# Order of the first loads and transposes, and the queue of the last store, in a gated linear-attention kernel

## The chip, the cores and the metric

The kernel runs on one core of a Trainium2 chip. The metric is the time of one execution in microseconds (us) as the device measures it.

## The reference, cut to what matters

```python
x = A_x                                             # (1, 2048, 1024) bf16
g = sigmoid((x * gate_w).sum(-1, keepdims=True))
a = linear_attention(x, A_wqkv, A_wo)               # 32 heads of 32; phi(q), phi(k), num / den, then @ wo
b = one_token_ffn(x, B_w_r, B_w_gate, B_w_up, B_w_down)   # FFN of the one token with the largest x @ w_r
return g * a + (1 - g) * b                          # (1, 2048, 1024) bf16
```

The start of the kernel computes K = x @ wk for the first two tiles of 128 tokens, for which x has to be transposed. The end writes the last 128 rows of the output.

## The kernel before

The transfers at the start, all from SyncE's queue. Tiles 0 and 1 of x come plain and are transposed on TensorE; later tiles are transposed by the transfer itself. A "K row" is 128 rows of the K weights (256 KB, as much as one x tile).

```python
load_x(0, 1)
load_k(0)
load_x(1, 1)
for c in range(1, KC):          # KC = 8
    load_k(c)
v_cut = D + 32 * (VH[0] + VH[1])
sp.dma_start(out=wkv[:, :, v_cut : 2 * D], in_=wqkv_v[:, :, D + v_cut : 3 * D])   # the V piece, 640 KB
...
```

TensorE's work on them, in program order. `warm` issues dummy matmuls that keep the array busy; `first_mm(t, c0, c1)` does two matmuls of 512 columns for each K row c of tile t.

```python
warm(N_WARM)                    # 6 dummies of 512 columns
...
unit_T(0)                       # 8 transposes of tile 0, copied out by VectorE and ScalarE
warm(3, 128)
first_mm(0, 0, 1)
wps = ps_ffn.tile([P, 16], BF, tag="f")
pe.transpose(wps[:], wrg_rows[:], ident[0:16, 0:16])     # router and gate rows
dve.tensor_copy(wkv[:, :, 2 * D : 2 * D + 2], wps[:].rearrange("p (w c) -> p c w", w=2))
unit_T(1)
for c in range(1, KC):
    first_mm(0, c, c + 1)
    if c < KC - 1:
        first_mm(1, c - 1, c)
...
for t in range(3):
    unit_V(t, 2, ps_t, "t")     # the first matmuls that need the V piece
```

The last row tile is computed and stored in three pieces of 512, 384 and 128 columns:

```python
for c0, cw in cols:
    ...                         # 8 matmuls
    dve.scalar_tensor_tensor(ot[:, c0 : c0 + cw], ps[:, 0:cw], gate[:, t : t + 1], xg[:, c0 : c0 + cw], ...)
    if t == NT - 1:
        nc.sync.dma_start(out=out2d[t * P : (t + 1) * P, c0 : c0 + cw], in_=ot[:, c0 : c0 + cw])
```

## Time and profile before

| | before |
|---|---|
| median of 6 runs (range) | 249.16 us (248.55 to 249.42) |
| span of the profiled run | 247.02 us |
| TensorE's share of the chain that ended last | 97% |
| first matmul of K row 1 / first V matmul | 6.54 / 13.01 us |
| end of VectorE's last instruction | 243.81 us |
| from there to the end of the span ("the tail") | 3.20 us |

TensorE has no gap worth the name from 1 us to 243 us. So a change can win only at what delays TensorE at the start, or in the tail. The prediction shows the lines.

### The profile page before, as it was taken

The page shows a single profiled execution, that of the slowest core. Times are in us where ns is not written, and L with a number is a line of the kernel's source. Part 1 is how long each engine was busy: PE and PEld are TensorE (multiplying, and loading weights), DVE is VectorE, ACT ScalarE, POOL GpSimd, SP SyncE. Part 2 cuts the span into 40 slices and gives each one's busy share as a digit, 9 for nine tenths or more (in the row PEclk, how much of TensorE's full clock was granted, in tenths as well). Part 3 has the DMA queues.
Part 4 walks back from the last instruction along what each step waited for, and adds up shares of the span by engine and source line. Part 5 has one row for each costly group of instructions (what it writes and reads, how often), then busy time and mean ns, then how long its engine had stood idle before and what let it go on. Part 6 is the DMA issues. An engine that isn't in the chain of part 4 may idle for free.

```text
span 247.0 us, 4867 instructions
## 1 busy us (share of the span) xinstructions
PE 240.8 (97%) x1898; PEld 123.6 (50%) x1923; DVE 172.7 (70%) x264; ACT 127.6 (52%) x215; POOL 52.5 (21%) x100
## 2 busy tenths in 40 slices
PE   8999999999999999999999999999999999999994
PEld 3466756654554554554554555544443444444442
DVE  0053124379984989845989999996789999954342
ACT  3195343355566376545555555668887633333300
POOL 6000000400000100000003300101666689950000
PEclk9999999999999999999999999999999999999999
DMA  6999995499969993599699690000004754464122
GB/s 207 343 239 195 267 392 151 108 326 337 281 194 292 341 290 88 149 312 384 224 345 340 230 280 3 3 4 21 0 3 127 204 182 148 155 190 166 48 82 86
DMA packets 46311, 47.78 MB, mean 193 GB/s; under 512 B 16776, under 2 KB 35472, under 8 KB 46224
## 3 DMA queue, kind: packets, MB, share of 16 engines
q1 hardware_dynamic: 45648, 46.28, 61.5%
q0 software_dynamic: 608, 1.19, 1.7%
q8 instruction: 15, 0.25, 0.5%
q14 instruction: 8, 0.07, 0.1%
q10 hardware_dynamic: 32, 0.00, 0.0%
HBM read 39.33 MB, written 8.39 MB: 193 GB/s over the span
## 4 chain that ended last, share of the span: by engine, by line
PE 97%; issue 1%; DVE 0%; DVEq 0%
PE ps L83 88%; PE first L83 3%; PE kvacc L83 2%; PE warm_ps L83 1%; PE red L83 1%; PE dps L83 1%; PE pst L83 1%; PE pm L83 1%; DVE ot L83 0%; PE yps L83 0%; PE pt L83 0%; DVEq L739 0%; PE hps L83 0%; PE rps L83 0%; PE wps L83 0%
## 5 line engine op out<-in xcount | busy, mean ns | idle before, releaser
L83 PE MATMUL ps<-wkv,xT 128*128 128x352 bf16 (+2 forms) x600 | 106.1, 334 | 0.4
L83 PEld LDWEIGHTS <-xT 128*128 128x128 bf16 x640 | 62.1, 98 | 49.1 <-issue 0.3
L83 ACT ACTIVATE u<-ps 128x512 f32<-128x512 f32 x60 | 35.9, 598 | 46.3 <-PE ps L83 45.7
L83 PE MATMUL ps<-xT,wq 128*128 128x512 bf16 x245 | 57.3, 379 | 0.6 <-issue 0.2
L83 PE MATMUL ps<-m_sb,pq_all 128*128 128x512 bf16 (+2 forms) x259 | 55.4, 373 | 0.3
L83 ACT ACTIVATE e<-u 128x512 f32<-128x512 f32 x64 | 40.3, 630 | 2.0
L83 PEld LDWEIGHTS <-pq_all 128*128 128x128 bf16 x264 | 25.4, 98 | 30.2 <-issue 0.7
L641 POOL TENSOR_TENSOR pq_all<-pq_all,rb 128x512 bf16<-128x512 bf16 x32 | 36.4, 1171 | 12.1 <-DVE rb L83 11.5
L83 PEld LDWEIGHTS <-wq 128*128 128x128 bf16 x256 | 24.5, 98 | 28.2 <-issue 1.0
L83 DVE SCALAR_TENSOR_TENSOR gacc<-wt,hcol,gacc 128x1024 f32<-128x1024 bf16 x27 | 34.5, 1278 | 0.4
L83 DVE SCALAR_TENSOR_TENSOR ot<-ps,gate,xg 128x512 bf16<-128x512 f32 (+2 forms) x33 | 23.9, 738 | 14.3 <-PE ps L83 13.1
L83 DVE SCALAR_TENSOR_TENSOR gacc<-wt,xs_f,gacc 128x2048 f32<-128x2048 bf16 x14 | 32.8, 2345 | 0.2
L83 ACT ACTIVATE xg<-xt,omg 128x1024 f32<-128x1024 bf16 x16 | 18.2, 1147 | 26.8 <-DVE ot L83 25.8
L83 DVE SCALAR_TENSOR_TENSOR pq_all<-ps,e 128x512 bf16<-128x512 f32 x32 | 21.9, 687 | 11.3 <-ACT e L83 11.3
L83 DVE SCALAR_TENSOR_TENSOR pk<-ps,e 128x512 bf16<-128x512 f32 x28 | 19.0, 686 | 11.8 <-ACT e L83 11.6
L83 DVE STREAM_SHUFFLE rb<-rdp 128x512 f32<-128x512 f32 x32 | 22.8, 753 | 0.0
L83 ACT CAST vt<-ps 128x352 bf16<-128x352 f32 x32 | 14.4, 453 | 11.4 <-PE ps L83 11.1
L214 POOL MEMSET vt<- 128x22 bf16 x16 | 3.7, 432 | 75.7 <-PE kvacc L83 75.2
L83 ACT CAST vc<-ps 128x320 bf16<-128x320 f32 x16 | 6.5, 428 | 7.3 <-PE ps L83 7.3
L83 DVE COPY rg<-ps 128x2 f32<-128x2 f32 x16 | 2.5, 159 | 10.2 <-ACT vc L83 10.1
L355 POOL DMA_DIRECT2D xs<-in_A_x_dram x1 | 0.7, 711 | 39.3 <-DVE sig L83 39.3
L83 DVE SCALAR_TENSOR_TENSOR pk<-first,e 128x512 bf16<-128x512 f32 x4 | 2.8, 692 | 7.9 <-ACT e L83 7.9
(100 smaller groups left out, 94.9 us busy)
## 6 DMA issues: line engine op xcount, KB each, us to landing
wt<-in_B_w_down_dram SPq DMA_DIRECT2D x14, 512.0 KB, 4.9
wt<-in_B_w_gate_dram SPq DMA_DIRECT2D x8, 512.0 KB, 7.6
wt<-in_B_w_up_dram SPq DMA_DIRECT2D x8, 512.0 KB, 8.3
xt<-xp SPq DMA_DIRECT2D x16, 256.0 KB, 2.7
out_dram<-ot SPq DMA_DIRECT2D x15, 256.0 KB, 2.0
wt<-in_B_w_gate_dram SPq DMA_DIRECT2D x8, 384.0 KB, 7.6
wt<-in_B_w_up_dram SPq DMA_DIRECT2D x8, 384.0 KB, 7.2
wkv<-in_A_wqkv_dram SPq DMA_DIRECT2D x8, 256.0 KB, 4.4
```

The lines of the kernel that those rows point to most:

```text
L83: inst = fn(*a, **k)
L214: nc.gpsimd.memset(vt_t[t][:, :, 32:33], 1.0)
L355: nc.gpsimd.dma_start(out=xs8[:], in_=x2d[bass.ds(idx_val, 1), :].rearrange("o (c p) -> (o c) p", p=P))
L641: nc.gpsimd.tensor_tensor(sl, sl, rb[:], op=ALU.mult)
```

## The change

Its intent: have both plain x tiles early, so that TensorE does all its transposes before the first K row is needed and never waits for tile 1; and let an idle engine issue the last store at once, where SyncE was still busy with the store before. The diff also moves the PSUM buffer (PSUM is TensorE's output memory) of the small transpose, `wps`, from the dummies' pool to that of the other transposes.

```diff
--- before.py
+++ after.py
@@ -134,9 +134,8 @@
         sp.dma_start(out=wkv[:, c, 0:D], in_=wqkv_v[:, c, D : 2 * D])
 
     load_x(0, 1)
-    load_k(0)
     load_x(1, 1)
-    for c in range(1, KC):
+    for c in range(KC):
         load_k(c)
     v_cut = D + 32 * (VH[0] + VH[1])
     sp.dma_start(out=wkv[:, :, v_cut : 2 * D], in_=wqkv_v[:, :, D + v_cut : 3 * D])
@@ -275,12 +274,13 @@
                 kv_mm(first[t][nb], t, nb, c, c + 1)
 
     unit_T(0)
-    warm(3, 128)
-    first_mm(0, 0, 1)
-    wps = ps_ffn.tile([P, 16], BF, tag="f")
+    wps = ps_t.tile([P, 16], BF, tag="t")
     pe.transpose(wps[:], wrg_rows[:], ident[0:16, 0:16])
     dve.tensor_copy(wkv[:, :, 2 * D : 2 * D + 2], wps[:].rearrange("p (w c) -> p c w", w=2))
+    warm(2, 128)
     unit_T(1)
+    warm(4, 128)
+    first_mm(0, 0, 1)
     for c in range(1, KC):
         first_mm(0, c, c + 1)
         if c < KC - 1:
@@ -703,7 +703,7 @@
             dve.scalar_tensor_tensor(ot[:, c0 : c0 + cw], ps[:, 0:cw], gate[:, t : t + 1],
                                            xg[:, c0 : c0 + cw], op0=ALU.mult, op1=ALU.add)
             if t == NT - 1:
-                nc.sync.dma_start(out=out2d[t * P : (t + 1) * P, c0 : c0 + cw], in_=ot[:, c0 : c0 + cw])
+                (nc.scalar if c0 + cw == D else nc.sync).dma_start(out=out2d[t * P : (t + 1) * P, c0 : c0 + cw], in_=ot[:, c0 : c0 + cw])
         if t < NT - 1:
             nc.sync.dma_start(out=out2d[t * P : (t + 1) * P, :], in_=ot[:])
         if t == 0:
```

## The prediction

> **What bounds the kernel now.** I read the page from the top: busy shares, then the chain that ended last, then the timeline of the first 14 us and of the last 5 us, because the diff touches only those two ends. The page says that TensorE is the bound nearly everywhere:
>
> ```profile
> span 247.0 us, 4867 instructions
> PE 240.8 (97%) x1898; PEld 123.6 (50%) x1923; DVE 172.7 (70%) x264; ACT 127.6 (52%) x215; POOL 52.5 (21%) x100
> ...
> PE 97%; issue 1%; DVE 0%; DVEq 0%
> ```
>
> The second line gives busy time and share per engine, the last one the chain of work that ended last by engine. TensorE has 97% of both, so what counts is what delays TensorE at the start, and what comes after its last matmul. The chain in order of time shows no gap over 0.1 us in the first 13 us:
>
> ```profile
> 1.02 2.72 PE warm_ps L83 x6
> 3.74 1.02 PE pst L83 x8
> 4.76 0.32 PE warm_ps L83 x3
> 5.08 0.85 PE first L83 x2
> 5.93 0.12 PE wps L83
> 6.05 0.59 PE pst L83 x8
> 6.64 4.59 PE first L83 x21
> ```
>
> Columns: start, us, what, count. The reader should divide. The two first matmuls of 512 columns take 0.85 us, 427 ns each (half clock). The 8 transposes of tile 0 take 1.02 us, 128 ns each with the last one's drain; those of tile 1 take 0.59 us, 74 ns each. So the array went over to full speed near 6.0 us; single starts of the second group, 80 ns and then 55 ns apart, say the same. From 6.54 us, when the matmul of K row 1 starts in the timeline, to 13.01 us, when the first V matmul starts, lie 30 matmuls (2 times 7 rows for tile 0, 2 times 8 for tile 1; one record is missing): 6.47 / 30 = 216 ns each, full speed with no stall. No later K row holds TensorE up.
>
> The arrivals come from the issue starts in the timeline plus the time to landing of each issue, taken in narrow windows of the tiles' view:
>
> ```profile
> 0.98 0.40 SPq L83 DMA_DIRECT2D xnat<-in_A_x_dram  x1
> 1.44 0.42 SPq L83 DMA_DIRECT2D wkv<-in_A_wqkv_dram  x1
> 1.90 0.45 SPq L83 DMA_DIRECT2D xnat<-in_A_x_dram  x1
> 2.39 3.75 SPq L83 DMA_DIRECT2D wkv<-in_A_wqkv_dram  x8
> ```
>
> x tile 0 lands 2.7 us after its issue, at 3.68 (TensorE starts on it at 3.72); K row 0 2.8 after, at 4.24; x tile 1 3.8 after, at 5.70; K row 1 4.1 after, at 6.49; row 2 4.3 after, at 7.16; row 7 5.7 after, at 10.9. Each is there before its use (tile 1 at 5.98, row 2 at about 7.4, row 7 at about 11.7), except row 1: it lands at 6.49 and its matmul starts at 6.54. It is the one transfer that TensorE just about waits for: the last transpose of tile 1 starts at 6.42 and would have let it start at about 6.48.
>
> The other end is the timeline after 242.3 us:
>
> ```profile
> 242.94 0.88 DVE L83 SCALAR_TENSOR_TENSOR ot<-ps,gate,xg 128x384 bf16<-128x384 f32 x2 [0.49 <-PE ps L83]
> ...
> 243.58 0.33 SPq L706 DMA_DIRECT2D out_dram<-ot  x1
> ...
> 244.01 0.38 SPq L706 DMA_DIRECT2D out_dram<-ot  x1
> ```
>
> The first line is two VectorE instructions, 242.94 to 243.56 and 243.56 to 243.82. The middle piece goes out at 243.58, 0.02 us after its data. The last piece goes out at 244.01, 0.19 us after its data, because SyncE is still at the middle one until 243.91 and needs some 0.1 us more. The DMA view gives 1.5 us from issue to landing for the last piece and 1.6 for the middle one: landings at 245.5 and 245.2. The span ends 1.5 us later, with nothing else of the kernel.
>
> **What the Trainium skill says.** "TensorE: Matmul & The Clock Gate", Part 1: the array starts at half clock and is let up to full after about 3.4 us of sustained work, in a free-running window, so the moment changes from run to run; it is a budget of time and not of matmuls. The trace agrees with the two speeds (427 and 216 ns for 512 columns); the change of speed comes 5.0 us after the first matmul, which fits a window that began some time after it. The same page gives N/2.4 + 2.5 ns for a matmul of N columns at full speed, 216 ns for 512, as measured here. "DMA: Bandwidth & Descriptors", Issuing engines are not separate DMA queues: issuing from another engine saves only the sequencer's issue time. That is the change at the end, and the trace shows that time as 0.33 to 0.38 us an issue. The same page, Anatomy of one DMA, puts most of the fixed 2 us of a transfer into confirming the last byte; the 1.5 us of this 32 KB piece fits, and another queue doesn't shorten it.
>
> **The change part by part.** Start, transfers: x tile 1 and K row 0 change places in one queue; both are 256 KB. So I give x tile 1 the old landing of row 0 (4.24) and row 0 the old one of tile 1 (5.70). Row 1 and all later ones keep theirs, as the bytes ahead of them are the same.
>
> Start, TensorE: moved are the small transpose of the router rows (it cost about 0.26 us, from the end of the matmuls before it at 5.72 to 5.98) and the 8 transposes of tile 1, now ahead of the first two K matmuls. Added are 6 dummy matmuls of 128 columns in place of 3: 3 x 128 = 384 columns more. Nothing useful is removed. The new path, at half clock 107 ns for 128 columns: tile 0's transposes 3.72 to 4.57; router transpose to 4.83; two dummies to 5.04; tile 1's transposes, 8 x 107, to 5.90 (their second PSUM buffer is freed by ScalarE's copy, which ends at 5.37, and is needed at about 5.47: no wait); then four dummies, one at half clock and three at full (56 ns), to about 6.17; then two K matmuls of row 0, 2 x 216 = 0.43, to 6.60. Row 0 is there at 5.70. Row 1's matmul starts at 6.60 instead of 6.54: 0.06 us later. From there the same 30 matmuls follow at 216 ns. The effect is bounded on both sides. As row 1 lands at 6.49 in both, nothing can start earlier than 6.53: the gain is at most 0.01 us. And the extra work is 384 columns, 0.16 us at full clock, which is what it costs if the clock goes up late (the work done before that moment is the same in both, and what is left over is done at full clock). So the start costs 0.06, between 0 and 0.16.
>
> Router copy: VectorE's copy of the router columns comes earlier, between the two tiles' copies; VectorE is idle there, so nothing.
>
> End: ScalarE has nothing left to do, and can start the last issue some 0.03 us after the data, at 243.85 instead of 244.01: 0.16 us saved. The landing is at 245.35 instead of 245.5, still after the middle piece at 245.2, so all of it shows. Another 0.15 is the most that could come beyond it, as the middle piece then ends last.
>
> Sum: +0.06 - 0.16 = -0.10 us, 0.04%: 249.1 becomes 249.0.
>
> **The rivals.** (1) The small transpose waits for its own data, as it now comes a microsecond earlier (4.57 instead of 5.86). For it: its weight load shows 0.84 us idle put down to "issue", and starts 0.14 us after the array was free, so something the profile doesn't name may have held it. Against it: the packets of that ScalarE queue are all moved by 3.1 us in the DMA view, and other transfers were done a few tenths after their last small packet. If it did wait until 5.8, TensorE would idle 1.2 us and might go over to full speed later: 250 to 251 us. I give this one in twelve. (2) x tile 1 lands later than 4.24, say at 5.3, since the queue serves several transfers at once. Then tile 1's transposes end at 6.1 and the start costs 0.2 us more. (3) The two queues share what makes descriptors, so the last piece gains nothing, or ScalarE's issue is slower (its first took 0.58 us, its second 0.28, against 0.40 for SyncE's first): the end then gives 0 and the total is 249.2. (4) Early data keeps TensorE busier in the runs in which the clock goes up early. There the kernel before waits for tile 1 until 5.70; but then both versions wait for row 1 at 6.49, so it gives nothing. (5) The order of instructions in the middle, which the program leaves partly free, comes out differently in the build. TensorE is 97% busy there, so that would cost or give tenths, but I can't see it from the profile.
>
> **Range and chances.** The three runs before lie between 249.04 and 249.42, so the moment of the clock and the chip alone make 0.2 either way, and my working spans -0.3 to +0.4. That gives 249.0, with 248.4 to 249.7 for 8 in 10. A 2% change is 5 us, more than all that happens outside TensorE's gapless stretch at both ends (the start before K row 1 is 6.5 us, the end after the last matmul some 3.5). Faster by over 2% 0.01, within 2% 0.98, slower 0.01.
>
> **What would show it.** In the profile after: x tile 1 landing near 4.3 and K row 0 near 5.7; row 1 still near 6.5; its first matmul between 6.5 and 6.7; the first V matmul 6.47 us after that; the last output issued from ScalarE's queue some 0.03 us after VectorE's last instruction, inside SyncE's issue of the middle piece; and the span from the end of VectorE's last instruction shorter by 0.16 from 3.2 us. I am wrong if row 1 itself lands earlier or later, if a gap appears before the small transpose or tile 1's transposes, if the clock goes up at another moment in a regular way, or if the middle of the kernel is ordered anew.

## The result, and the profile after

| | before | after |
|---|---|---|
| median of 6 runs (range) | 249.16 us (248.55 to 249.42) | 249.11 us (248.74 to 249.61) |
| span of the profiled run | 247.02 us | 247.48 us |
| first matmul of K row 1 | 6.54 us | 6.78 us |
| first V matmul | 13.01 us | 13.38 us |
| end of VectorE's last instruction | 243.81 us | 244.27 us |
| tail | 3.20 us | 3.21 us |

The ratio is 1.000, with a 95% interval of 0.9984 to 1.0017: the same.

The page of the changed kernel, busy times and the chain by engine:

```profile
span 247.5 us, 4896 instructions
PE 242.8 (98%) x1926; PEld 124.3 (50%) x1926; DVE 172.7 (70%) x264; ACT 127.6 (52%) x215; POOL 52.6 (21%) x100
...
PE 98%; DVE 0%; DVEq 0%; issue 0%
```

TensorE still bounds it. (Its 28 instructions more are mostly records that the trace before lacks: the program has 3 dummies more.) The chain in order of time, to be held against the seven lines in the prediction:

```profile
3.74 0.99 PE pst L83 x8
4.73 0.12 PE wps L83
4.85 0.33 PE warm_ps L83 x2
5.18 0.85 PE pst L83 x8
6.03 0.43 PE warm_ps L83 x4
6.46 6.96 PE first L83 x32
```

Both groups of transposes now take 0.85 us or more, so both run at half clock. The first K matmul follows all of them, at 6.25 us. The V matmuls then wait, which the kernel before did not show (timeline, weight loads; the bracket is the idle time ahead and what ended it):

```profile
13.38 0.66 PEld L83 LDWEIGHTS <-xT 128*128 128x128 bf16 x6 [0.45 <-DMA wkv<-in_A_wqkv_dram]
```

The end of the changed kernel (SPq and ACTq are the issuing sides of SyncE and ScalarE):

```profile
243.40 0.88 DVE L83 SCALAR_TENSOR_TENSOR ot<-ps,gate,xg 128x384 bf16<-128x384 f32 x2 [0.49 <-PE ps L83]
244.04 0.33 SPq L706 DMA_DIRECT2D out_dram<-ot  x1
244.31 0.39 ACTq L706 DMA_DIRECT2D out_dram<-ot  x1
```

The last issue starts 0.03 us after VectorE's end at 244.27 and inside SyncE's issue, as predicted. The span nevertheless ends 3.206 us after VectorE, against 3.205 before.

One profile of each kernel says little here: the two differ by 0.46 us, the medians by 0.05 the other way. So the experiments were read by the times of a few events in each trace. Each row below is one trace. "Full clock" is the moment at which the trace's record of the clock begins, which agrees with the change in the spacing of matmuls (in one trace 427, 260, then 216 ns apart about 10.07 us). The V column is the first V matmul. From there to VectorE's end lie 230.8 to 231.0 us in all 14 traces, so what the start loses or gains arrives at the end.

| kernel | K row 1 landed | its first matmul | full clock | V landed | V | VectorE's end | tail |
|---|---|---|---|---|---|---|---|
| before | 6.49 | 6.54 | 6.09 | 12.95 | 13.01 | 243.81 | 3.20 |
| before_again | 7.06 | 7.10 | 5.92 | 13.23 | 13.57 | 244.49 | 3.19 |
| end_only | 6.73 | 6.78 | 6.43 | 12.90 | 13.25 | 244.16 | 3.20 |
| after | 6.62 | 6.78 | 6.44 | 13.34 | 13.38 | 244.27 | 3.21 |
| after_again | 6.57 | 7.01 | 6.85 | 12.93 | 13.49 | 244.38 | 3.20 |
| after_third | 6.54 | 6.58 | 5.38 | 13.12 | 13.16 | 243.94 | 3.21 |
| start_only | 6.72 | 6.76 | 4.56 | 12.86 | 13.24 | 244.10 | 3.20 |
| no_dummies | 6.76 | 6.80 | 4.97 | 12.89 | 13.28 | 244.20 | 3.23 |
| more_dummies | 7.21 | 8.34 | 6.76 | 13.35 | 14.82 | 245.71 | 3.21 |
| order_only | 6.25 | 6.70 | 4.71 | 12.78 | 13.18 | 244.07 | 3.19 |
| swap_only | 6.60 | 7.86 | 10.07 | 13.15 | 15.43 | 246.44 | 3.20 |
| swap_filled | 7.45 | 7.88 | 5.44 | 13.42 | 14.39 | 245.26 | 3.20 |
| two_act | 7.21 | 7.25 | 6.70 | 13.24 | 13.72 | 244.57 | 2.96 |
| all_act | 6.93 | 6.98 | 4.03 | 13.33 | 13.45 | 244.34 | 2.85 |

### The profile page after: what moved, and what is told of

It is laid out like the page before. It is cut to its first block, busy times and chain, and to the rows that moved or that the text cites. A ratio compares the mean times of both kernels' runs of the same rounds, so it can differ in the third digit from the quotient of the medians.

```text
span 247.5 us, 4896 instructions
## 1 busy us (share of the span) xinstructions
PE 242.8 (98%) x1926; PEld 124.3 (50%) x1926; DVE 172.7 (70%) x264; ACT 127.6 (52%) x215; POOL 52.6 (21%) x100
## 4 chain that ended last, share of the span: by engine, by line
PE 98%; DVE 0%; DVEq 0%; issue 0%
PE ps L83 88%; PE first L83 3%; PE kvacc L83 2%; PE warm_ps L83 1%; PE red L83 1%; PE pst L83 1%; PE dps L83 1%; PE pm L83 1%; DVE ot L83 0%; PE yps L83 0%; PE pt L83 0%; DVEq L739 0%; PE hps L83 0%; PE rps L83 0%; PE wps L83 0%; PE xs_ps L83 0%
## 5 line engine op out<-in xcount | busy, mean ns | idle before, releaser
L83 PE MATMUL ps<-xT,wq 128*128 128x512 bf16 x256 | 58.3, 379 | 0.0
```

What stands on the lines that cost most here:

```text
L83: inst = fn(*a, **k)
```

## The experiments

The theory at this point: the start costs the dummies' columns and is otherwise ruled by chance (the moment of the clock), and in the tail something later than the landing swallows the gain. Rivals: the change itself moves the clock; the later K and V landings in its profile belong to it; the tail does gain and the single trace hides it. All outputs are right.

### Both kernels again: before_again, after_again

No edit. Five rounds each, together with the next two.

> The kernel before, unchanged, once more. Theory 'chance': the moment at which the array goes to full clock wanders by itself by some tenths of a us or more (6.1 in the first profile of this kernel, 6.4 in that of the changed one), and each us of it is worth 0.5 us of time; so this copy shows another moment than 6.1, and the end of VectorE's last instruction less half of that moment stays at 240.77 within 0.1. The tail after it stays 3.20. Rival 'the change moves the clock': this copy shows 6.1 again within 0.1. Ratio 1.000 within 0.002.

> The changed kernel, unchanged, once more. 'Chance': the clock goes up at another moment than 6.44; end of VectorE's last instruction less half of that moment is 241.05 as in the first profile if the 0.4 us later landings of K row 7 and the V piece (11.38 and 13.34 against 10.96 and 12.95) belong to the change, and about 240.93 (the 384 dummy columns alone, 0.16) if they were chance. 'The change moves the clock': 6.4 again. Ratio 1.000 within 0.002.

Measured: medians 248.99 and 249.17 us; ratios to the kernel before 0.9978 (0.9942 to 1.0013) and 0.9978 (0.9943 to 1.0013). The intervals are wide because two of the 11 runs of the kernel before took 251.02 and 250.91 us. The changed kernel went to full clock at 6.85 instead of 6.44 us. So the moment wanders with no change of the program; over all traces it lies between 4.0 and 6.9 where TensorE had no long gap before it. The later landings were chance, too: the V piece landed at 12.93 in this trace of the changed kernel and at 13.23 in that of the kernel before.

The reckoning "half of the clock's moment plus a constant" fell: the kernel before ends at 244.49 with a clock at 5.92, which gives 241.54 and not 240.77. (after_again gives 240.95, near the 240.93 expected of chance, but a reckoning that fails for one kernel supports nothing for the other.) The reason is in its timeline:

```profile
5.88 0.18 PE L83 MATMUL wps<-ident,wrg_rows 16*128 16x16 bf16 x1
6.24 0.62 PE L83 MATMUL pst<-ident,xnat 128*128 128x128 bf16 x8 [0.18 <-DMA xnat<-in_A_x_dram]
7.10 6.63 PE L83 MATMUL first<-wkv,xT 128*128 128x512 bf16 x29 [0.24 <-DMA wkv<-in_A_wqkv_dram]
```

The first bracket shows a wait for x tile 1, which landed at 6.20 instead of 5.68. That wait is what the change is meant to remove. The second bracket shows a further wait for K row 1, which makes the first one harmless: with tile 1 early, TensorE would have waited for K row 1 all the same.

### One part each: start_only, end_only

The changed kernel with the old end, and the kernel before with the new one:

```diff
# start_only, against after
-                (nc.scalar if c0 + cw == D else nc.sync).dma_start(out=out2d[...
+                nc.sync.dma_start(out=out2d[...
# end_only, against before: the opposite
```

> The start of the change with the old end. My sum of the start is a cost of 0.16 us for the dummy columns and up to 0.13 for a wait at the first V matmul: ratio 1.0006 to 1.0012, hardly to be told from 1. End of VectorE's last instruction less half of the clock's moment 240.93 to 241.05. The tail after it 3.20, the last issue 0.19 us after the data.

> The end of the change with the old start. My prediction: the last issue 0.03 us after its data and the tail 3.05 instead of 3.20, ratio 0.9994. Rival 'something later ends it': the last issue is 0.16 us earlier, but the tail is 3.20 again as in the changed kernel's first profile (3.206 against 3.205). End of VectorE's last instruction less half of the clock's moment 240.77, as before.

Measured: start_only 248.88 us, ratio 0.9976 (0.9942 to 1.0010); end_only 249.16 us, ratio 0.9993 (0.9958 to 1.0027). Neither is to be told from 1; the ratio of start_only lies below the 1.0006 to 1.0012 expected, inside the noise, and its VectorE end less half of the clock's moment is 241.83, outside the expected 240.93 to 241.05. The traces tell why. The chain of start_only, followed back from its end, leaves TensorE in the first microseconds and runs through one transfer:

```profile
1.90 0.45 SPq L83
2.35 0.04 issue
2.39 4.33 DMA wkv<-in_A_wqkv_dram
6.72 0.04 issue
6.76 4.05 PE first L83 x18
```

The third line is K row 1, issued at 2.39 and landed at 6.72. The array was at full clock by 4.56, TensorE was done with everything else, and the six dummies cost nothing. So the moment of the clock and the dummies count only where TensorE is later than that landing.

In end_only the last issue is 0.03 us after its data, and the tail is 3.196 us. The prediction for the end (3.05) is refuted, the rival (3.20) confirmed. The expectation for VectorE's end missed by 0.17 for the reason just told.

### What the dummies cost: more_dummies, no_dummies

```diff
# more_dummies, against after            # no_dummies, against after
     unit_T(1)                           -    warm(2, 128)
-    warm(4, 128)                             unit_T(1)
+    warm(28, 128)                       -    warm(4, 128)
     first_mm(0, 0, 1)                        first_mm(0, 0, 1)
```

> The changed kernel with 28 dummy matmuls of 128 columns after tile 1's transposes in place of 4: 24 x 128 = 3072 columns more. If a dummy costs its columns at full clock as I reckoned (24 x 56 ns = 1.33 us), the matmul of K row 1 starts 1.3 us later than the 6.8 to 7.0 of the changed kernel (at about 8.1 to 8.4), nothing waits for K rows or the V piece after that, and the whole is 1.1 to 1.3 us longer (ratio 1.005). If the start is bound by transfers and dummies are free, it starts by 7.1 and the ratio is 1.000.

> The changed kernel without its six short dummies. If 'the later of two' sets the start (K row 1's landing + 0.04 us, or TensorE's own work), the matmul of K row 1 now starts 0.04 us after that row lands, wherever that falls (6.5 to 7.1), so 0 to 0.3 us earlier than in the changed kernel: ratio 0.999 to 1.000, not to be told from 1. If the dummies are needed to bring the clock up, the array goes to full clock later than 7 us and the start is later than 7.1.

Measured: more_dummies 250.41 us, ratio 1.0051 (1.0031 to 1.0071), K row 1's matmul at 8.34; as expected. The 24 more dummies cost about their columns: the start moves by 1.33 to 1.56 us against after and after_again, 1.33 expected. no_dummies: K row 1 landed at 6.76 and its matmul started at 6.80, so the later of the two did set the start. Ratio 1.0027 (0.9990 to 1.0064), drawn up by one run of four at 250.77 us. Without the dummies TensorE idles:

```profile
4.87 0.68 PE L83 MATMUL pst<-ident,xnat 128*128 128x128 bf16 x8
6.15 7.29 PE L83 MATMUL first<-wkv,xT 128*128 128x512 bf16 x32 [0.60 <-DMA wkv<-in_A_wqkv_dram]
```

Here the array was already at full clock (4.97) and the 0.60 us did no harm. What such a gap does when it comes earlier is the next pair's subject.

### The two halves of the start: swap_only, order_only

```diff
# swap_only, against before: only the transfers
     load_x(0, 1)
-    load_k(0)
     load_x(1, 1)
-    for c in range(1, KC):
+    for c in range(KC):
# order_only, against after: old transfers and old end, new order and dummies on TensorE
```

> The kernel before with only the two transfers exchanged: x tile 1 ahead of K row 0, TensorE's order and dummies as before. Its first K matmuls come before tile 1's transposes and now wait for K row 0 until 5.4 to 6.0 instead of starting at 4.9; then 0.4 to 0.9 us of matmuls, 0.26 for the small transpose and 0.5 to 0.9 for tile 1: K row 1's matmul starts at 7.2 to 7.9, 0.4 to 1.1 us later than in the kernel before. Ratio 1.002 to 1.004. Rival 'exchange is free': by 7.1.

> The changed order of TensorE's work and its dummies with the old order of transfers and the old end. Tile 1's transposes are reached at 5.0 and wait for tile 1 until 5.4 to 6.2; then 0.5 to 0.9 us of transposes, 0.2 to 0.4 of dummies and 0.43 of matmuls: K row 1's matmul at 6.9 to 7.6, 0.1 to 0.6 us later than the changed kernel's 6.8 to 7.0. Ratio against before 1.001 to 1.002. So the two parts of the start are of use only together, and together give nothing over the kernel before.

Measured: swap_only 250.40 us, the four runs 251.18, 249.61, 251.25 and 248.53; ratio 1.0031 (0.9980 to 1.0083). K row 1's matmul came at 7.86, inside the expected range, yet VectorE ended at 246.44, 1.9 to 2.6 us later than in all traces but the two with many dummies. TensorE in that trace:

```profile
4.59 0.53 PE L83 MATMUL warm_ps<-const-bfloat16-1.0 128*128 128x128 bf16 x3
5.96 1.01 PE L83 MATMUL first<-wkv,xT 128*128 128x512 bf16 x2 [0.84 <-DMA wkv<-in_A_wqkv_dram]
6.91 0.19 PE L83 MATMUL wps<-ident,wrg_rows 16*128 16x16 bf16 x1
7.03 1.03 PE L83 MATMUL pst<-ident,xnat 128*128 128x128 bf16 x8
7.86 7.74 PE L83 MATMUL first<-wkv,xT 128*128 128x512 bf16 x30
```

The first K matmuls wait 0.84 us for K row 0. After it everything is at half clock (the transposes take 1.03 us), and stays so until 10.07. From 7.86 to the first V matmul at 15.43 lie 7.57 us, where other kernels need 6.47. That was not in my expectation. By the Trainium skill, "TensorE: Matmul & The Clock Gate", Part 1, the clock goes up after a busy window of some 3.4 us. My inference, which the page does not state, is that a gap inside a window puts the clock off by a whole one. 10.07 is 3.4 us past 6.66, a moment inside the 4.0 to 6.9 of the other traces, so it fits.

order_only: 249.26 us, ratio 1.0036 (0.9993 to 1.0080). It waits 0.42 us for tile 1, as expected, but its K row 1 matmul came at 6.70, below my 6.9: full clock was early (4.71). One of its four runs took 251.22 us.

### The gap filled, and the changed kernel once more: swap_filled, after_third

```diff
# swap_filled, against swap_only
-    warm(3, 128)
+    warm(12, 128)
```

> The kernel with only the two transfers exchanged, whose TensorE stood idle from 5.1 to 6.0 and went to full clock only at 10.1, now with 12 dummies of 128 columns in place of 3, which fill that idle time. Theory 'a gap loses a window': the array goes to full clock between 4.4 and 7.9 in each run, none is over 250.2 us, and the median is about 249.3 although it does more work than the exchange alone (median 250.4, two runs of four over 251). Rival 'the order itself is slow': median 250 or more, with some runs over 250.5 again.

> The changed kernel a third time, beside more runs of the kernel before. So far 2 of 36 runs with the old order of the start were over 250.5 us, and none of 18 with the new one and its dummies. If the new order guards against a lost window, none of these is over 250.2 and a few of the kernel before are; if the two were chance, both show some or none. Ratio 1.000 within 0.002; tail 3.20.

Measured: swap_filled 249.43 us (248.70 to 250.00), ratio 1.0014 (0.9997 to 1.0031). In its profile K row 0 is waited for again and landed later still, but the dummies run to 5.87 us, past the moment of the full clock at 5.44:

```profile
4.63 1.24 PE L83 MATMUL warm_ps<-const-bfloat16-1.0 128*128 128x128 bf16 x12
6.79 0.59 PE L83 MATMUL first<-wkv,xT 128*128 128x512 bf16 x2 [0.92 <-DMA wkv<-in_A_wqkv_dram]
7.31 0.18 PE L83 MATMUL wps<-ident,wrg_rows 16*128 16x16 bf16 x1
7.42 0.62 PE L83 MATMUL pst<-ident,xnat 128*128 128x128 bf16 x8
```

The transposes take 0.62 us, and none of six runs is over 250.0. So with more work on TensorE the median is 1 us lower than with the exchange alone; but two of the four runs of swap_only were as fast, the runs are of different rounds, and the two intervals overlap. The lost window is supported, not shown: it was seen in one trace, the only one with a gap before the change of clock, and no trace of the other long runs was kept. That this clock was late by chance, as it may have been in the long runs of the kernel before, is not excluded.

after_third: 249.27 us, ratio 1.0012 (0.9999 to 1.0026). None of its runs is over 250.2, but none of the kernel before is either. In all, 2 of 47 runs with the old start and its dummies (before, before_again, end_only) were over 250.5 us, and none of 31 with the new one. That is too few to say that the change guards against such runs; it stays open.

### The tail: all_act, two_act

The trace also records SyncE's own waits and drains at the end of the program. Here they are from record 204 on, counted from 0, with their starts in us after VectorE's last instruction (an excerpt of the trace's records, four kernels side by side):

```
record   before         after          two_act        all_act
204      wait  1.42     wait  1.77     drain 1.99     wait  2.21
205      wait  1.75     wait  1.85     drain 2.06     drain 2.31
206      wait  1.84     drain 1.92     wait  2.22     wait  2.79  (last)
207      wait  2.23     drain 2.30     drain 2.63
208      drain 2.31     wait  2.57     wait  2.90  (last)
209      drain 2.41     drain 2.66
...
```

Between the end of record 206 and the start of 207 SyncE stands still for 0.363 us before and 0.367 us after. In the 12 traces of 211 or 213 SyncE records this time is 0.362 to 0.368 us and always in front of number 207, whatever that record does. It looked bound to a place in SyncE's program. The test is to make that program shorter:

```diff
# all_act, against after                 # two_act, against after
-  (nc.scalar if c0 + cw == D else ...   -  (nc.scalar if c0 + cw == D else ...
+  (nc.scalar if True else ...           +  (nc.scalar if c0 > 0 else ...
```

> All three pieces of the last row from ScalarE's queue. Theory 'SyncE's program': in all profiles so far SyncE stands still for about 0.37 us before the same one of its records, number 207 counted from 0, whatever that one is (a wait in the kernels with the old end, a drain in those with the new one), and this hides the earlier landing. Here SyncE has two records fewer for each piece taken away, 207 in all, so the pause falls behind its last one: the tail from VectorE's last instruction to the end goes from 3.20 to 2.7 to 2.9. ScalarE issues one after the other, so the last issue is again 0.2 us after the data. Rival 'something fixed at the end of the program' (a confirmation, a barrier): 3.2 again. Ratio 0.998 to 0.999 by the first, 1.000 by the rival.

> The last two pieces from ScalarE's queue: SyncE has 209 records. By 'SyncE's program' the pause now falls before the third drain, behind the first barrier, and costs about 0.3 instead of the 0.4 us it costs with the old end: tail 3.0 to 3.15. By the rival 3.2.

Measured: the tail of all_act is 2.85 us, within the 2.7 to 2.9 expected, and that of two_act 2.96, a little less than the 3.0 to 3.15 expected. In all_act no record 207 exists. In two_act the 0.39 us stand in front of 207, now the third drain. The gain is not that of an earlier issue, as ScalarE now issues all three pieces itself (timeline of all_act):

```profile
243.46 0.87 DVE L83 SCALAR_TENSOR_TENSOR ot<-ps,gate,xg 128x384 bf16<-128x384 f32 x2 [0.49 <-PE ps L83]
244.11 0.85 ACTq L706 DMA_DIRECT2D out_dram<-ot  x2
```

Its last issue is 0.19 us after the data, as in the kernel before, and its last landing 1.78 us after it (1.73 before); still the program ends 0.35 us sooner after VectorE. The timing goes the same way without settling it: all_act 248.88 us, ratio 0.9997 (0.9981 to 1.0012), beside 1.0012 (0.9999 to 1.0026) for the changed kernel of the same rounds. The difference of 0.0015 is 0.37 us, as much as the tails differ, but the intervals overlap, and 0.998 to 0.999 was expected. So all_act has the shortest tail of all versions, and no gain over the kernel before that is clear of noise. Not tested is a program with more idle records and the old queues, which would separate the number of records from the move of the stores. What SyncE does in those 0.36 us, the trace doesn't say. Fetching the next stretch of its program is only a guess: no packet of the instruction queues falls into the pause in any of the 13 traces. But record 79, 128 places earlier, has such a pause as well, 0.45 us in all 14 traces, with the semaphore that it waits for there over 3 us before.

## Why the prediction was right or wrong

**The time and the class were right.** 249.0 was predicted, 249.11 measured, within 248.4 to 249.7. That says little about the working: the range is wide enough for no change at all and for the failure of either term. The two terms of the sum fared differently.

**The bound: right, and stronger than told.** "The one transfer that TensorE just about waits for" is K row 1: in all three traces with the old start its first matmul comes 0.04 us after that row's landing. In six traces with the whole new start (after, after_again, after_third, start_only, all_act, two_act) it is the same 0.04 in four. This is why tile 1's earlier landing gains nothing.

**The landings: partly right.** x tile 1 came at 4.30 us in the changed profile (4.24 predicted) and K row 0 at 5.96 (5.70). But "row 1 and all later ones keep theirs" treated one trace's landing as a constant. Row 1 landed between 6.25 and 7.45 over all traces: a spread of 1.2 us, twenty times the effect I computed. Four traces with the old order of transfers have a mean of 6.63, ten with the new one 6.86; whether that is the exchange or chance is open.

**The start term, +0.06 us: the mechanism held, its size can't be told.** K row 1's matmul follows the later of two times, the landing plus 0.04 and TensorE's own work. The new start pushed TensorE past the landing in two of the six traces, by 0.12 and 0.40 us, those with full clock at 6.44 and 6.85; in the other four by nothing. In the changed profile that gave 6.78, just outside the 6.5 to 6.7 named as a sign. Nor is all of the 0.40 the change's: by an estimate, the kernel before, whose transposes of tile 1 start at 5.98 and take 0.83 us at half clock (swap_only), would at a clock of 6.85 have come to K row 1 at 6.81, 0.2 past this landing too. So that the mean of the six, 0.09, is near the 0.06 is no confirmation. I assumed full clock at 6.0 as in the one profile; its moment ran from 4.0 to 6.9.

**A wait that I did not foresee.** "No later K row holds TensorE up" was true for K rows, but the V piece is next in line: it landed only 0.06 us before its use in the profile before. In the changed profile the first V matmul is 0.13 us later than 6.47 us past K row 1's, and in after_third 0.11.

**The end term, -0.16 us: wrong, it is 0.00.** The step that failed reads: "still after the middle piece at 245.2, so all of it shows." The issue did move by 0.16. The landing moved by only 0.07 (1.73 to 1.66 us after the data), as the time from issue to landing grew from 1.54 to 1.63. The middle piece, issued no later, landed later by the same 0.09 (1.39 to 1.41 us after VectorE's end in the six traces with the old end, 1.48 to 1.51 in the six with the new one; two_act and all_act are counted apart). The other 0.07 was lost after the landing: from there to the end of the span lie 1.473 to 1.474 us in all six traces with the old end, and 1.543 to 1.544 in all six with the new one. So the end does follow the landing, but this time is not the same in the two programs; I had taken it as one constant. Its pause in front of record 207 is as long in both (0.363 and 0.367 us). What grew is the rest: with the new end three records instead of one lie between the wait for the last landing and the pause, and the drain that now comes right after the pause takes 0.12 us and not 0.01. In two_act this time is 1.176 us, in all_act, without the pause, 1.071. That the tails (3.19 to 3.21 with the old end, 3.20 to 3.23 with the new one) come out equal is thus two losses that happen to add up to the gain.

**The rivals.** (1), the small transpose waiting for its data: no, it starts 0.14 us after the array is free in the changed kernel, as it did before. (2), tile 1 landing at 5.3: no, it lands between 4.30 and 4.54 in the ten traces with the new order of transfers. (3) named the outcome of the end, nothing gained, with a partly other cause: ScalarE's issue took no longer than SyncE's (0.39 against 0.38 us). (5): apart from the lines of the diff, the order of instructions is the same on every engine. What I lacked among the rivals is a gap in TensorE's work before the clock has gone up. It would explain why the exchange alone cost the profiled run of swap_only about 2 us and not the 0.8 us of the wait; as said, it is not shown.

## What to carry to other kernels

Before counting what an earlier transfer saves, find the transfer that is waited for last; here tile 1 came 1.4 us earlier, and K row 1 still set the start. A landing, and the moment of the full clock, are draws and not constants: take a few traces of the same kernel before explaining tenths of a microsecond. An earlier last issue is worth only what is left of it at the landing (0.07 of 0.16 us here) and after the closing instructions (0.00). Here, moving all three stores off the engine that closes the program, which makes its program shorter, was worth more: 0.35 us of tail, in one trace.

## What the Trainium skill lacked or had wrong

- "TensorE: Matmul & The Clock Gate", Part 1, puts the change of speed at about 4 us into sustained work, half a microsecond more or less. Here, with the first matmul at 1.02 us in every trace, it came 3.0 to 5.8 us after it where TensorE had no long gap before it, and 9.1 us after it in the trace with 0.84 us of idle time from 5.1 to 6.0 us. The least, 3.0 us, is shorter than the 3.4 us of sustained work in the page's table. The page warns of idle time longer than a window; it doesn't say how busy a window has to be. If the gap was the cause, which is not shown, a quarter of a window was enough to lose it.
- "DMA: Bandwidth & Descriptors", Anatomy of one DMA, gives a fixed cost and a rate for transfers that GpSimd issues, but no spread, and no such pair for SyncE's queue. The same 256 KB, issued by SyncE at 2.4 us behind the same 768 KB, landed between 6.25 and 7.45 us.
- No page has the stand-still of SyncE near the end of a program: 0.36 to 0.39 us ahead of its record 207 in 13 traces, and a tail of 2.85 instead of 3.20 us where the program ended before that record. None says either that the time from the last landing to the end depends on which engine issues the last stores: 1.47 us with none from ScalarE, 1.54 with one, 1.18 with two and 1.07 with three.
